# SwiGLU block in fp32: value and gate products split into three reduced-precision products, with the gating on GpSimd

## The chip, the cores and the metric

The kernel runs on one core of one Trainium2 chip. The metric is device time in microseconds (us). Engines in the profile: PE (TensorE, matmul), PEld (its weight loads), DVE (VectorE), ACT (ScalarE), POOL (GpSimd) and SP (SyncE, whose queue starts most transfers).

## The reference

A polysketch attention feeds a SwiGLU feed-forward block. q, k and v are fp32. The sketches S1, S2 and the three weights come as float64; the kernel narrows them to fp32 in its first 65 us (lines L216 to L239), beside the first batch.

```python
def phi(x):                                   # x: (4 batches, 4 heads, 1088, 32)
    a = np.einsum('rd,bhsd->bhsr', S1, x)     # r = 8
    b = np.einsum('rd,bhsd->bhsr', S2, x)
    return np.einsum('bhsi,bhsj->bhsij', a, b).reshape(*x.shape[:-1], r * r)
q_p, k_p = phi(q), phi(k)
kv = np.einsum('bhsf,bhsd->bhfd', k_p, v)
z = np.sum(k_p, axis=2)
num = np.einsum('bhsf,bhfd->bhsd', q_p, kv)
den = np.einsum('bhsf,bhf->bhs', q_p, z)[..., None] + 1e-06
x = (num / den).transpose(0, 2, 1, 3).reshape(4352, 128)

g = x @ w_gate                                # 128 x 1536
silu = g * (1.0 / (1.0 + np.exp(-g)))
val = x @ w_val                               # 128 x 1536
out = silu * val @ w_out                      # 1536 x 128
```

## The kernel before

The 4352 tokens stand as columns of `xT`, 128 partitions deep. Each batch of 1088 tokens is three blocks of 384, 384 and 320 columns; the 1536 hidden values are 12 chunks of 128. One chunk of one block is a *unit*: a gate product, a value product, Silu and the product of both, and later a *down* product that adds the unit to the block's sum. There are 144 units. An fp32 matmul of the program appears in the profile as two matmul instructions.

```python
    free_banks = ["g0", "g1", "g2", "acc"]      # one bank of 512 fp32 columns each
    def bank(tag=None):                         # round robin over the free banks
        if tag is None:
            tag = free_banks[turn[0] % len(free_banks)]
            turn[0] += 1
        return psum.tile([P, TB], FP32, tag=tag, name="bank")
    def wide(tag):                              # "a" and "b": two banks each, for the attention
        return psum.tile([P, 2, TB], FP32, tag=tag, name=tag)

    LAG = 2
    def unit(i, j, late=False, between=(None, None)):
        t0, n = blocks[i]
        g, u = bank(), bank()
        for o, w in ((g, wg), (u, wv)):
            ... # between
            nc.tensor.matmul(o[:, 0:n], w[:, j, :], xT[:, t0 : t0 + n], start=True, stop=True)  # L773
        sg = fpool.tile(...)
        nc.scalar.activation(sg[:, 0:n], g[:, 0:n], AF.Silu)                                   # L779
        ... # hj: a place of hbuf
        todo.append((i, j))
        ... # late units of the first batch: copied by ScalarE, multiplied on GpSimd (L796)
            nc.vector.tensor_tensor(out=hj[:, 0:n], in0=sg[:, 0:n], in1=u[:, 0:n], op=ALU.mult) # L790

    def down():
        i, j = todo.pop(0)
        ...
        nc.tensor.matmul(acc[i][:, 0:n], wo[:, j, :], hidden[i, j][:, 0:n],
                         start=(j == 0), stop=(j == NCH - 1))                                  # L804
        ...
        if j == NCH - 1:
            store(i, n)                         # VectorE transposes (L833), then the output's transfers
```

The attention of the later batches is a generator whose pieces are laid between the units: `parts_of(n)` lays n pieces, `group()` lays pieces up to the next point at which TensorE's attention products stand together, and those products. The pieces are mostly VectorE's: feature products (L324), spread products and sums (L679, L686), transposes (L710, L274, L509). The feature sums are GpSimd's (L494), the numerators TensorE's (L730).

```python
    while todo:                                 # end of the first batch
        for _ in range(min(3, len(todo))):
            down()
        if ahead[0] != "first":
            parts_of(1)
    ...
    for b in range(1, B):                       # batches 2 to 4
        for z in range(3 * NCH):
            i, j = z // NCH, z % NCH
            if (b, z) in ((1, NCH), (2, 0), (2, 2 * NCH)):
                group()
            unit(3 * b + ((0, 2, 1)[i] if b == B - 1 else i), j)
            for _ in range(2):
                if len(todo) > LAG:
                    down()
            parts_of(2 if b == 1 and z in (0, 4, 6, 7, 8) else 1)
    ps = wide("a")[:, 0, 0:D]
    for j in range(NCH):                        # the last 128 tokens, straight into the output's form
        if todo and j % 4 == 0:
            down()
        straight(ps, j)                                                                        # L819
```

Of the kernel before, what the change touches and what calls it, by code (L numbers as in the profile page):

```python
# [6 lines left out]

FP32 = mybir.dt.float32
I32 = mybir.dt.int32
U32 = mybir.dt.uint32  # L10
I64 = mybir.dt.int64
AF = mybir.ActivationFunctionType
ALU = mybir.AluOpType
# [5 lines left out]
def kernel(  # L19
# [28 lines left out]
    nc = tc.nc  # L48
# [9 lines left out]
    NCH = Dff // P  # L58
# [25 lines left out]
    free_banks = ["g0", "g1", "g2", "acc"]  # L84
    turn = [0]

    def bank(tag=None):
        if tag is None:
            tag = free_banks[turn[0] % len(free_banks)]
            turn[0] += 1  # L90
        return psum.tile([P, TB], FP32, tag=tag, name="bank")

    def wide(tag):
        return psum.tile([P, 2, TB], FP32, tag=tag, name=tag)

    nc.scalar.preload_act_table(AF.Silu)

# [157 lines left out]
    def run(*gens):  # L255
        for g in gens:
            for _ in g:
                pass
# [242 lines left out]
    def turns(b):  # L501

        for c in kpieces:
            turn_k(*c)
            if c[1] == NC and b + 1 < B:
                load_k(b + 1)
            yield
        for x0, x1 in ((0, 4 * kpieces[0][1]), (4 * kpieces[0][1], 4 * NC)):
            nc.vector.transpose(out=qT[:, x0:x1, :], in_=qld[:, x0:x1, :])  # L509
            if x1 == 4 * NC and b + 1 < B:  # L510
                load_q(b + 1)
            yield
# [19 lines left out]
    def attentions():  # L532

        yield from turns(1)
        kp, qp = wide("a"), wide("b")
        for ps, products in ((kp, key_products), (qp, query_sketches)):
            for i, c in enumerate(kpieces):
                products(ps[:, i, :], *c)
        ka = apool.tile([P, NC * H, R], FP32, tag="kas", name="kas")
        qab = apool.tile([P, 2, NC * H, R], FP32, tag="qab", name="qab", bufs=2)
        fac = None, qab

        def sketch(ps, i):  # L550
            c0, c1 = kpieces[i]
            return ps[:, i, 0 : 64 * (c1 - c0)].rearrange("p (x t r) -> p x t r", t=2, r=R)

        for i, (c0, c1) in enumerate(kpieces):
            nc.scalar.copy(ka[:, H * c0 : H * c1, :], sketch(kp, i)[:, :, 0, :])
        phk = apool.tile([P, NC, H, R, R], FP32, tag="phk", name="phk")
        for n, (i, c0, c1) in enumerate(((0, 0, 3), (0, 3, 5), (1, 5, 7), (1, 7, 9))):
            first = H * (c0 - kpieces[i][0])
            kb = sketch(kp, i)[:, first : first + H * (c1 - c0), 1, :]
            key_features(phk, (ka[:, H * c0 : H * c1, :], kb), c0, c1)  # L560
            if n < 2:
                q0, q1 = kpieces[n]
                nc.scalar.copy(
                    qab[:, :, H * q0 : H * q1, :], sketch(qp, n).rearrange("p x t r -> p t x r")
                )
            if n % 3 != 1:
                yield
        zs = feature_sums(phk)
        for i, _ in enumerate(turns(2)):
            if i % 2:  # L570
                yield
        kvz = wide("a")
        values(kvz[:, 0, :], phk, zs)
        kq = wide("b")
        fac2, copies = sketches([
            (0, NC - 1, kq[:, 0], kq[:, 1]),
            (NC - 1, NC, kvz[:, 1, 0 : 2 * F], kvz[:, 1, 2 * F : 4 * F]),
        ])
        spread = spread_out(1, kvz[:, 0, :])
        for _ in range(4):  # L580
            yield
            run_copies(copies, 1)
        step = query_step(1, fac, spread)
        yield from step(0, 3)
        numerators(1, spread, 0, 3)
        yield "first"
        yield from step(3, NC)
        phk = hbuf[:, NH - 6 :, :].rearrange("p s (n h i j) -> p (s n) h i j", h=1, i=R, j=R)
        phk = phk.rearrange("p (c h) o i j -> p c (h o) i j", h=H)
        yield from features(phk, fac2, ())  # L590
        zs = feature_sums(phk)
        yield from turns(3)
        yield "pe"
        numerators(1, spread, 3, NC)
        kv = bank()
        values(kv, phk, zs)
        kp, qp = wide("a"), wide("b")
        fac3, copies = sketches([(c0, c1, kp[:, i], qp[:, i]) for i, (c0, c1) in enumerate(kpieces)])
        spread = spread_out(2, kv)
        run_copies(copies, 2)  # L600
        yield
        run_copies(copies, 2)
        yield
        yield from features(phk, fac3, ())
        zs = feature_sums(phk)
        yield from query_step(2, fac2, spread)(0, NC)
        yield "pe"
        numerators(2, spread, 0, NC)
        kv = bank()
        values(kv, phk, zs)  # L610
        spread = spread_out(3, kv)
        for _ in range(4):
            yield
        yield from query_step(3, fac3, spread)(0, NC)
        yield "pe"
        numerators(3, spread, 0, NC)
        yield

    def run_copies(copies, n):
        for f, *args in copies[:n]:  # L620
            f(*args)
        del copies[:n]
# [139 lines left out]

    lates = []

    def unit(i, j, late=False, between=(None, None)):


# [3 lines that stand above are left out]
            if between[0] and w is wv:  # L771
                between[0]()
            nc.tensor.matmul(  # L773
                o[:, 0:n], w[:, j, :], xT[:, t0 : t0 + n], start=True, stop=True
            )
        sg = fpool.tile(
            [P, BW], FP32, tag="sgl" if late else "sg", name="sg", bufs=6 if late else 3
        )
        nc.scalar.activation(sg[:, 0:n], g[:, 0:n], AF.Silu)  # L779
        slot_of[i, j] = slots.pop(0)  # L780
        hj = hbuf[:, slot_of[i, j], :]
        hidden[i, j] = hj
        todo.append((i, j))
        if late:
            if between[1]:
                between[1]()
            nc.scalar.copy(hj[:, 0:n], u[:, 0:n])
            lates.append((hj[:, 0:n], sg[:, 0:n]))
        else:
            nc.vector.tensor_tensor(  # L790
                out=hj[:, 0:n], in0=sg[:, 0:n], in1=u[:, 0:n], op=ALU.mult
            )
# [5 lines left out]
    def down():  # L798

        i, j = todo.pop(0)  # L800
        n = SPLIT if i == LAST else blocks[i][1]
        if j == 0:
            acc[i] = bank("g1" if i == 1 else "acc")
        nc.tensor.matmul(  # L804
            acc[i][:, 0:n],
            wo[:, j, :],
            hidden[i, j][:, 0:n],
            start=(j == 0),
            stop=(j == NCH - 1),
        )  # L810
        if i != LAST:
            hidden.pop((i, j))
            slots.append(slot_of[i, j])
        if j == NCH - 1:
            store(i, n)

    def straight(ps, j):

# [130 lines left out]
    def parts_of(n):  # L949

        for _ in range(n):
            if ahead[0] not in ("pe", "end"):
                ahead[0] = next(att, "end")

    def group():
        while ahead[0] != "pe":
            ahead[0] = next(att)
        ahead[0] = next(att, "end")
# [42 lines left out]
    order = [(i, j) for i in range(3) for j in range(NCH)]  # L1001
    for z, (i, j) in enumerate(seq):
        if z == 17:
            free_banks.pop()
            turn[0] %= 4
        unit(i, j)
        for p in parts.get(z, ()):
            part(*p)
        if z in (24, 25, 26):
            catch_up()  # L1010
        if z == 6:
            load_k(1)
            load_v(1, [nc.sync] * 4)
            load_q(1)
        if z >= 17:
            todo.remove(order[0])
            todo.insert(0, order.pop(0))
            down()
        if z >= 17:
            parts_of(1)  # L1020
    todo.sort()
    while todo:
        for _ in range(min(3, len(todo))):
            down()
        if ahead[0] != "first":
            parts_of(1)
    while ahead[0] != "first":
        parts_of(1)

    slots[:] = range(NH - 6)  # L1030

    for b in range(1, B):
        for z in range(3 * NCH):
            i, j = z // NCH, z % NCH
            if (b, z) in ((1, NCH), (2, 0), (2, 2 * NCH)):
                group()
            unit(3 * b + ((0, 2, 1)[i] if b == B - 1 else i), j)
            for _ in range(2):  # L1040
                if len(todo) > LAG:
                    down()
            parts_of(2 if b == 1 and z in (0, 4, 6, 7, 8) else 1)
    ps = wide("a")[:, 0, 0:D]
    for j in range(NCH):
        if todo and j % 4 == 0:
# [40 lines left out]
```

## Time and profile before

| | |
|---|---|
| time, median of 3 (lowest, highest) | 305.9 us (305.71, 306.23) |
| span of the profiled execution | 304.3 us |
| batch 1 ends, its remaining downs included | 92.5 us |
| start of the first unit after the group in batch 2 | 120.1 us |
| attention products before batch 3 | 163.1 us |
| attention products within batch 3, for batch 4 | 212.2 us |
| the last 16 matmuls begin | 298.7 us |

The times of the stages are from the timeline of the profile. A busy share in the page is an average over the whole span; the view by windows gives busy times in stretches. In a line of a group, the count stands after the x, then the busy us, the mean ns of one, and the idle time of the engine just before, with what ended it. In a timeline line the first number is the start and the second the length; `x2` merges two instructions in a row. A matmul's length contains the drain of the array, so the pace of a stream of matmuls is the distance of their starts. An idle time is put down to the engine that released the instruction last.

### The profile page before, as it was taken

To read this page: it belongs to the slowest core of one execution; us is meant where nothing else is said; L and a number is where in the kernel's file an instruction comes from. 1 tells how busy PE (TensorE), PEld (TensorE's weight loads), DVE (VectorE), ACT (ScalarE), POOL (GpSimd) and SP (SyncE) were. 2 spreads that over 40 slices of the span, in tenths; PEclk is the share of its full clock that TensorE was granted. 3 is DMA by queue.
4 is the path that set the end of the run, shared out by engine and by line. 5 is a ranking of instruction groups with operands and counts; after the bars stand their busy time and mean duration, and the time that the engine had idled before them with its cause. 6 is when DMAs were issued, how large, how long until landed. Compare 5 with 4: busy or idle time off the path is not lost.

```text
span 304.3 us, 5402 instructions
## 1 busy us (share of the span) xinstructions
PE 298.0 (98%) x2179; PEld 190.3 (63%) x2179; DVE 170.0 (56%) x334; ACT 93.8 (31%) x219; POOL 37.9 (12%) x54
## 2 busy tenths in 40 slices
PE   8899999999999999999999999999999999999995
PEld 7545566657565556556666655555676556676664
DVE  3997988692536991788932478822423322333321
ACT  3566764422102222322222222222322222222230
POOL 3216222174000050070000000000000000000000
PEclk9999999999999999999999999999999999999999
DMA  7563490404511000400100200100100100100101
GB/s 195 150 193 106 119 302 7 149 15 149 113 28 22 0 2 22 108 0 0 26 3 2 49 0 0 28 0 0 23 5 0 22 1 2 26 0 2 21 0 26
DMA packets 26136, 14.57 MB, mean 48 GB/s; under 512 B 18688, under 2 KB 24192, under 8 KB 26112
## 3 DMA queue, kind: packets, MB, share of 16 engines
q1 hardware_dynamic: 25456, 14.13, 18.5%
q8 instruction: 17, 0.28, 0.4%
q10 hardware_dynamic: 656, 0.10, 0.2%
q14 instruction: 7, 0.06, 0.1%
HBM read 11.41 MB, written 2.23 MB: 45 GB/s over the span
## 4 chain that ended last, share of the span: by engine, by line
PE 97%; DVE 1%; issue 0%; ACT 0%
PE bank L773 58%; PE bank L804 28%; PE bank L194 2%; PE a L730 1%; PE b L289 1%; PE bank L335 1%; PE a L819 1%; PE a L301 1%; PE bank L348 0%; PE bank L301 0%; PE a L392 0%; PE a L444 0%; PE a L335 0%; PE b L301 0%; PE b L730 0%
## 5 line engine op out<-in xcount | busy, mean ns | idle before, releaser
L790 DVE TENSOR_TENSOR hbuf<-sg,bank 128x384 f32<-128x384 f32 (+1 forms) x138 | 72.9, 529 | 99.5 <-PE bank L773 97.7
L779 ACT ACTIVATE sg<-bank 128x384 f32<-128x384 f32 (+1 forms) x144 | 68.0, 473 | 163.1 <-PE bank L773 159.9
L773 PE MATMUL bank<-xT,wg 128*128 128x384 f32 (+1 forms) x288 | 112.5, 472 | 0.0
L773 PE MATMUL bank<-xT,wv 128*128 128x384 f32 (+1 forms) x288 | 111.5, 469 | 0.2 <-DVE wv L239 0.2
L804 PE MATMUL bank<-hbuf,wo 128*128 128x384 f32 (+2 forms) x288 | 105.1, 460 | 0.0
L773 PEld LDWEIGHTS bank<-xT,wv 128*128 128x128 f32 x288 | 54.5, 190 | 33.7 <-DVE hbuf L790 0.9
L804 PEld LDWEIGHTS bank<-hbuf,wo 128*128 128x128 f32 x288 | 54.6, 190 | 32.0
L773 PEld LDWEIGHTS bank<-xT,wg 128*128 128x128 f32 x288 | 53.7, 190 | 32.2 <-issue 1.6
L494 POOL TENSOR_TENSOR zs<-hbuf 128x1024 f32<-128x1024 f32 x2 | 4.7, 2359 | 51.6 <-DVE hbuf L324 37.6
L833 DVE STREAM_TRANSPOSE o<-bank 128x384 f32<-128x384 f32 (+2 forms) x12 | 6.6, 549 | 7.8 <-PE bank L804 7.4
L679 DVE TENSOR_TENSOR phq<-spread,qab 128x768 f32<-128x768 f32 x9 | 9.7, 1075 | 0.5 <-DMA spread<-spread 0.5
L221 ACT ACTIVATE exp<-exp,rebias 128x384 int32<-128x384 int32 (+3 forms) x15 | 8.3, 551 | 2.4 <-DVE exp L216 1.7
L710 DVE STREAM_TRANSPOSE phT<-phq 128x768 f32<-128x768 f32 x9 | 8.7, 968 | 0.1
L686 DVE TENSOR_REDUCE dot<-phq 128x96 f32<-128x768 f32 x9 | 8.5, 947 | 0.1
L324 DVE TENSOR_TENSOR phq<-qab 128x768 f32<-128x768 f32 x9 | 8.5, 942 | 0.0
L747 ACT COPY xT<-a 128x64 f32<-128x64 f32 (+3 forms) x7 | 2.3, 367 | 18.2 <-PE b L730 11.8
L224 DVE SCALAR_TENSOR_TENSOR exp<-raw,exp 128x384 int32<-128x384 int32 (+2 forms) x14 | 7.0, 503 | 0.0
L230 DVE SCALAR_TENSOR_TENSOR man<-raw,man 128x384 f32<-128x384 uint32 (+2 forms) x14 | 6.9, 493 | 0.0
L222 ACT ACTIVATE man<-man 128x384 f32<-128x384 int32 (+3 forms) x15 | 6.8, 452 | 0.0
L494 POOL TENSOR_TENSOR zs<-zs 128x512 f32<-128x512 f32 (+1 forms) x6 | 6.6, 1101 | 0.5
L239 POOL TENSOR_TENSOR wg<-man,exp 128x384 f32<-128x384 f32 (+1 forms) x5 | 4.0, 805 | 18.2 <-DVE man L230 14.0
L274 DVE STREAM_TRANSPOSE kT<-kld 128x384 f32<-128x384 f32 (+2 forms) x9 | 5.9, 688 | 0.3 <-DMA kld<-in_k_dram 0.3
(127 smaller groups left out, 161.4 us busy)
## 6 DMA issues: line engine op xcount, KB each, us to landing
kld<-in_k_dram SPq DMA_DIRECT2D x4, 544.0 KB, 4.3
vld<-in_v_dram SPq DMA_DIRECT2D x12, 144.0 KB, 5.1
qld<-in_q_dram SPq DMA_DIRECT2D x3, 544.0 KB, 4.2
raw<-in_moe_w_out_dram SPq DMA_DIRECT2D x4, 384.0 KB, 4.9
out_dram<-o SPq DMA_DIRECT2D x28, 48.0 KB, 1.9
raw<-in_moe_w_gate_dram SPq DMA_DIRECT2D x3, 384.0 KB, 3.6
raw<-in_moe_w_val_dram SPq DMA_DIRECT2D x3, 384.0 KB, 3.3
out_dram<-o SPq DMA_DIRECT2D x16, 40.0 KB, 1.7
```

Source lines behind the costliest of these rows:

```text
L221: nc.scalar.activation(e[:], e[:], AF.Relu, bias=rebias[: shape[0], :], scale=8.0)
L224: nc.vector.scalar_tensor_tensor(out=e[:], in0=hi, scalar=-(1 << 31), in1=e[:], op0=ALU.bitwise_and, op1=ALU.bitwise_or,)
L230: nc.vector.scalar_tensor_tensor(out=f, in0=lo, scalar=2.0**-52, in1=f, op0=ALU.mult, op1=ALU.add)
L324: engine.tensor_tensor(out=phk[:, c0:c1, :, :, :].rearrange("p c h i j -> p (c h) i j"), in0=ka.unsqueeze(3).to_broadcast([P, n, R, R]), i ...
L494: add = lambda o, a, b: nc.gpsimd.tensor_tensor(out=o, in0=a, in1=b, op=ALU.add)
L679: nc.vector.tensor_tensor(out=phq[:, c0:c1, :, :, :], in0=zrep.unsqueeze(1).to_broadcast([P, n, H, R, R]), in1=f.unsqueeze(3).to_broadcast ...
L686: nc.vector.tensor_reduce(out=dot[:, x, :], in_=phq[:, c0:c1, :, :, :].rearrange("p c h j i -> p (c h) j i"), axis=AX.X, op=ALU.add,)
L710: nc.vector.transpose(out=phT[:, :, :, c0:c1, :].rearrange("p h g c t -> p c (h g) t"), in_=phq[:, c0:c1, :, :, :].rearrange("p c h (g i) ...
L773: nc.tensor.matmul(o[:, 0:n], w[:, j, :], xT[:, t0 : t0 + n], start=True, stop=True)
L779: nc.scalar.activation(sg[:, 0:n], g[:, 0:n], AF.Silu)
L790: nc.vector.tensor_tensor(out=hj[:, 0:n], in0=sg[:, 0:n], in1=u[:, 0:n], op=ALU.mult)
L804: nc.tensor.matmul(acc[i][:, 0:n], wo[:, j, :], hidden[i, j][:, 0:n], start=(j == 0), stop=(j == NCH - 1),)
```

## The change

An fp32 number is cut into a part with 12 significant bits and a rest. The change's premise is that a matmul of type `float32r` multiplies such parts exactly. The value product is put together from three of them: with w = w1 + w0, x = x1 + x0 and beta = 4096, the parts are w1·x1, (beta·w0)·x0 and (w1 - beta·w0)·(x1 - beta·x0). A factor of 1 + 1/beta on the sum of the first two, and of -1/beta on the third, gives w1·x1 + w0·x1 + w1·x0 + w0·x0. The aim is to replace a full fp32 product on TensorE by three reduced ones, with the additions on engines that have time left.

In batches 2 and 3 the value product is split, in batch 4 the gate product too. Four units after two of the groups, and the last unit of all, stay as they were. The product of gate and value moves from VectorE to GpSimd in split units. Downs come up to five units after their unit, where it was two. From the 18th of the ordinary units of batch 1 on, banks are taken by age from all eight, of those that are not held, instead of round robin from three; the attention's double banks are held while it uses them.

```diff
+    PS = psum.tile([P, 8, TB], FP32, name="PS")
+    place = dict(g0=0, g1=1, g2=2, acc=3, a=4, b=6)
 ...
     def bank(tag=None):
-        if tag is None:
-            tag = free_banks[turn[0] % len(free_banks)]
+        if tag is not None:
+            i = place[tag]
+        elif oldest[0]:
+            i = min((i for i in used if i not in held), key=used.get)
+        else:
+            i = place[free_banks[turn[0] % len(free_banks)]]
             turn[0] += 1
 ...
+    def cut_weights(w):
+        for c, (w1, wb, wd) in enumerate(homes(w)):            # 4 pieces of 3 chunks
+            src = w[:, 3 * c : 3 * c + 3, :]
+            nc.scalar.activation(w1, src, AF.Copy, scale=CUT)
+            nc.gpsimd.tensor_tensor(out=low[:], in0=src, in1=whole(w1), op=ALU.subtract)
+            yield
+            nc.scalar.activation(wb, low[:], AF.Copy, scale=BETA)
+            nc.gpsimd.tensor_tensor(out=wd, in0=whole(w1), in1=whole(wb), op=ALU.subtract)
+            yield
+    def cut_tokens(i, engine=nc.gpsimd):
 ...
+        nc.scalar.activation(x1[:, 0:n], x, AF.Copy, scale=CUT)
+        engine.tensor_tensor(out=x0[:, 0:n], in0=x, in1=whole(x1[:, 0:n]), op=ALU.subtract)
+        yield
+        nc.vector.scalar_tensor_tensor(                        # xd = x1 - beta * x0
+            out=xd[:, 0:n], in0=whole(x0[:, 0:n]), scalar=-BETA, in1=whole(x1[:, 0:n]), ...)
+    def cut_unit(i, j, both=False):
 ...
+        for d, (_, _, wd) in zip(ds, parts):
+            nc.tensor.matmul(d, wd, xd, start=True, stop=True)
+        if not both:
+            nc.tensor.matmul(g, wg[:, j, :], xT[:, t0 : t0 + n], start=True, stop=True)
+        for w1, wb, _ in parts:
+            p = bank()[:, 0:n]
+            nc.tensor.matmul(p, w1, x1, start=True, stop=False)
+            nc.tensor.matmul(p, wb, x0, start=False, stop=True)
 ...
+        for d in ds:
+            nc.scalar.activation(s, d, AF.Copy, scale=-1.0 / BETA)
 ...
+        for p, s in zip(ps, sums):
+            nc.vector.scalar_tensor_tensor(
+                out=s, in0=p, scalar=1.0 + 1.0 / BETA, in1=s, op0=ALU.mult, op1=ALU.add)
+        nc.scalar.activation(sg, sums[0] if both else g, AF.Silu)
 ...
+        nc.gpsimd.tensor_tensor(out=hj[:, 0:n], in0=sg, in1=sums[-1], op=ALU.mult)
 ...
+    cutting = [cut_weights(wv), cut_weights(wg)]
     while todo:
 ...
+        for _ in range(2):
+            next(cutting[0], None)
 ...
+    line = [3 * b + k for b in range(1, B) for k in ((0, 2, 1) if b == B - 1 else range(3))]
+    END = len(line) * NCH
+    run(cut_tokens(line[0], nc.vector))
+    for y in range(END):
 ...
+        if (b, z) in ((1, NCH), (2, 0), (2, 2 * NCH)):
+            group()
+            if i not in x_parts:
+                run(cut_tokens(i, nc.vector))
+        if (b, z) in ((1, NCH), (1, NCH + 1), (2, 0), (2, 1)) or y == END - 1:
+            unit(i, j)
+        else:
+            cut_unit(i, j, both=b == B - 1)
+        lag = min(5, END - y + 1)
 ...
+        if b == 1 and z >= 3 * NCH - 18:
+            next(cutting[1], None)
+        if j == 4 and y // NCH not in (0, 2) and y + NCH < END:
+            coming_x = cut_tokens(line[y // NCH + 1])
+        if j in (4, 6):
+            next(coming_x, None)
```

## The prediction
> **What bounds the kernel now.** I read the page's engine totals and the chain of work that ended last first, since they say which engine's time is the kernel's time.
>
> ```profile
> PE 298.0 (98%) x2179; PEld 190.3 (63%) x2179; DVE 170.0 (56%) x334; ACT 93.8 (31%) x219; POOL 37.9 (12%) x54
> ...
> PE 97%; DVE 1%; issue 0%; ACT 0%
> ```
>
> TensorE is busy nearly all the time and is nearly all of the chain, so time is saved by giving it less to do and lost wherever it is made to wait. Next, the groups with shapes kept apart (line, engine, operation, count, then busy us and mean ns):
>
> ```profile
> L773 PE MATMUL bank<-xT,wg 128*128 128x384 f32 x192 | 78.5, 490 | 0.0
> ...
> L790 DVE TENSOR_TENSOR hbuf<-sg,bank 128x384 f32<-128x384 f32 x90 | 49.6, 551 | 63.0 <-PE bank L773 62.6 <-ACT sg L779 0.2
> L779 ACT ACTIVATE sg<-bank 128x384 f32<-128x384 f32 x96 | 47.2, 492 | 113.6 <-PE bank L773 110.4 <-DVE hbuf L790 3.2
> ...
> L796 POOL TENSOR_TENSOR hbuf<-hbuf,sg 128x384 f32<-128x384 f32 x6 | 5.9, 1003 | 0.0
> ```
>
> There are 96 units of 384 tokens and x192 matmuls: one fp32 matmul is two instructions. The mean of 490 ns contains the pipeline's drain; the pace is in the timeline (start, us, engine, ...):
>
> ```profile
> 251.28 0.81 PE L773 MATMUL bank<-xT,wv 128*128 128x384 f32 x2
> 251.48 0.49 ACT L779 ACTIVATE sg<-bank 128x384 f32<-128x384 f32 x1 [1.44 <-PE bank L773]
> 251.61 0.51 PEld L804 LDWEIGHTS bank<-hbuf,wo 128*128 128x128 f32 x2
> 251.93 0.81 PE L804 MATMUL bank<-hbuf,wo 128*128 128x384 f32 x2
> 252.20 0.56 DVE L790 TENSOR_TENSOR hbuf<-sg,bank 128x384 f32<-128x384 f32 x1 [1.38 <-PE bank L773]
> 252.25 0.51 PEld L773 LDWEIGHTS bank<-xT,wg 128*128 128x128 f32 x2
> 252.57 0.81 PE L773 MATMUL bank<-xT,wg 128*128 128x384 f32 x2
> ```
>
> Starts are 0.645 us apart, so one instruction takes 323 ns: two passes of 384 columns. A unit (gate, value, down) is 1.94 us. At 320 columns the same view gives 0.539 us a matmul, 1.62 a unit.
>
> Then the stages, in the view by windows (start:end, length, then busy us of PE, PEld, DVE, ACT, POOL):
>
> ```profile
> 92.50:116.00 23.50, 23.50 (x149) 13.63 (x151) 20.23 (x35) 6.01 (x13) 5.10 (x4) 1.00 0.05 8
> 116.00:143.00 27.00, 26.61 (x259) 16.85 (x248) 17.44 (x28) 7.83 (x19) 6.28 (x4) 1.00 0.16 37
> ...
> 187.00:211.00 24.00, 24.00 (x76) 14.20 (x75) 13.08 (x21) 5.89 (x12) 0.00 (x0) 1.00 0.06 9
> ...
> 276.00:298.20 22.20, 22.20 (x83) 14.92 (x82) 7.34 (x14) 5.89 (x12) 0.00 (x0) 1.00 0.05 8
> ```
>
> The average of 56% for VectorE hides that in the first stretch of the second batch (92.5 to 116) it is busy 20.2 of 23.5 us, while in the last batch (276 on) it is a third busy. The second batch is where an extra demand on it or on GpSimd can hurt. One more stretch of the timeline, for what happens when GpSimd and VectorE meet:
>
> ```profile
> 128.82 2.35 POOL L494 TENSOR_TENSOR zs<-hbuf 128x1024 f32<-128x1024 f32 x1 [14.02 <-PE bank L773]
> ...
> 129.46 0.55 DVE L790 TENSOR_TENSOR hbuf<-sg,bank 128x384 f32<-128x384 f32 x1 [0.78 <-PE bank L773]
> ...
> 129.93 2.06 DVE L679 TENSOR_TENSOR phq<-spread,qab 128x768 f32<-128x768 f32 x1
> ...
> 131.25 2.67 POOL L494 TENSOR_TENSOR zs<-zs 128x512 f32<-128x512 f32 x2
> ```
>
> L679 has a median of 951 ns; here it lasts 2.06, ending 0.8 after GpSimd's add ended at 131.17. The two GpSimd adds after it take 2.67 where an undisturbed pair takes 2.08 at 111.92. L790, with one operand in PSUM, is not slowed. So a VectorE operation with both operands in SBUF and a GpSimd operation exclude each other here.
>
> **What the Trainium skill says.** (1) "FP8 and Floating Point Precision", TensorE Precision Notes: true fp32 is four passes, reduced fp32 truncates the operand to about 22 bits. Two instructions of two passes agree with the four; a reduced matmul isn't in this trace. That it needs one pass is my inference: the built program after has 2317 matmul instructions against 2179, exactly one more for each of the 138 products that became three. (2) "TensorE: Matmul & The Clock Gate", Back-to-back issue gap: N/2.4 + 2.5 ns when warm. The trace agrees: 2 x 384/2.4 + 3 = 323. (3) "ScalarE: Activation LUTs", What ACT_TABLE_LOAD costs: 186 + 0.833 N ns, 506 at 384, and neighbours overlap by 93. The trace has 492 and starts of neighbours about 0.1 us closer than their lengths. (4) "GPSIMD Engine Reference", Specifications: its SBUF interfaces are shared with VectorE, with contention from instructions that have two SBUF inputs. The stretch just shown agrees, with 1.1 us lost by one of them.
>
> **The change, part by part.**
>
> *Removed from TensorE.* One reduced product is an estimated 384/2.4 + 3 = 163 ns, three are 489 against 646: 157 ns less. At 320 columns it is 3 x 136 = 408 against 539: 131 less. The weight loads should not be the limit: the last 16 matmuls (L819, 128 columns) begin about 0.11 us apart with a load each, and 0.11 is under 0.136. In batches 2 and 3 all but four units have a split value: 44 of 384 columns and 24 of 320, 44 x 0.157 + 24 x 0.131 = 10.1 us. In the last batch all but one unit have both split: 23 x 0.314 + 12 x 0.262 = 10.4 us. Sum: 20.5 us, a time of 285.4 if nothing waits.
>
> *Added elsewhere.* Each split product costs ScalarE one copy from PSUM (0.49) and VectorE one multiply-add (about the 0.55 of L790, whose place it takes for the value). The product with the gate goes to GpSimd, 1.00 us a unit by L796. Cutting the weights: 8 steps of ScalarE and 8 of GpSimd for each matrix; those of the value lie in the 15 us of down products before 92.5 and are hidden. Cutting tokens: 0.49 ScalarE, 0.5 to 1.0 on VectorE or GpSimd, 0.55 VectorE for each of nine blocks.
>
> *Last batch.* TensorE needs 6 x 0.163 + 0.646 = 1.62 us a unit. ScalarE has copy, copy, Silu, and the Silu waits for VectorE's sum: 0.49 + 0.04 + 0.55 + 0.04 + about 0.45 = 1.57, as the second copy lies beside the sum. At 320 columns: 1.36 against about 1.40. Balanced, so most of the 10.4 is kept; I take 1 us off, and 0.7 for the longer chain at the very end.
>
> *Middle batch (third).* GpSimd 1.0 and ScalarE 0.98 of 1.785 us, VectorE 13 of 24 us: kept.
>
> *Second batch, first stretch.* The cut of the first tokens stands on VectorE behind the store of the batch before (L833, 92.70 to 93.22), then two operations, so the first split product starts near 94.3 instead of 92.5, and VectorE's first sum near 95.6. From its first unit on, at 94.06, VectorE had 19.3 us of unbroken work in the kernel before. The work is the same now, with some 2 us for ten exclusions by GpSimd: 95.6 + 19.3 + 2 = 117, where it was 113.4. GpSimd's sums (5.6 us) follow. So the unit after the group starts near 121.7, where it was 120.1, with three more down products (1.9 us) still owed. Against the gain of 1.9 counted above this is a loss of about 5.4 us.
>
> *Second batch, second stretch.* For some thirteen units GpSimd has 13 products, one sum of 5.6, eight weight cuts and a token cut: 27.5 us, and some 5 us of VectorE's exclusive work between them. TensorE takes about 22. Downs five units behind give 5 x 1.785 less the chain of about 2.5, some 6.4 us, of slack: 32.5 - 22 - 6.4, a stall of 4. A ScalarE cut of the gate waits for GpSimd's step before it, which can pass the lag on to the sums; within the 4.
>
> *Banks.* The units now use the two double banks as well, so the attention products wait for a multiply-add to free them: an estimated 0.3 us at five places, 1.5.
>
> Sum: 305.9 - 20.5 + 1.7 + 5.4 + 4 + 1.5 = 298. The schedule has slack that I can't follow by hand, and the losses are counted one by one as if none covered another; I go one below, to 297.
>
> **The rivals.** *All of it lands* (TensorE stays the bound, 286 to 289): for it, 97% of the chain and the lag of five units; against it, VectorE's unbroken 19.3 us. *GpSimd and VectorE become the bound in the second batch* (about 297, my main line; 303 to 306 if the exclusions double): for it, the 2.06 us of L679; against it, that GpSimd's product starts just after VectorE has begun its next operation, which hides part. *Reduced products at half rate or with exposed weight loads*: at two passes a split costs three times 0.323 = 0.97 against 0.646, 138 x 0.3 = 42 us more, about 345. Against it, one instruction for each product; I give it 3%.
>
> **Range and chances.** The range spans the first rival's upper end to the second with doubled losses: 289 to 305. Under 299.8 is faster by 2%: most of the middle and all of the first rival, 0.68. Within 2%: 0.28. Slower: 0.04, almost all from the third.
>
> **What would show it.** Right: split products 0.163 us apart; TensorE's busy sum about 20 us less; idle TensorE time almost only between 92 and 165, waiting for VectorE before the first group and for GpSimd's products in the second stretch; the last batch near 1.62 and 1.4 us a unit. Wrong: starts over 0.2 us apart (a weight load or a second pass); a last batch clearly over 1.7 us a unit (ScalarE's chain); no idle time in the second batch (I overrated the exclusions, and it lands near 288); idle time in the third batch, which I take to be free of it.

## The result, and the profile after

The changed kernel takes 307.7 us (median of 4; 307.31 to 308.19) where the kernel before takes 305.8 beside it. The ratio is 1.006, with a 95% interval of 1.0046 to 1.0075. The prediction was 297, with a range of 289 to 305.

The page of the changed kernel, its engine totals, then the granted clock in 40 slices, then the shares of the chain of work that ended last:

```profile
PE 288.5 (94%) x2317; PEld 207.1 (68%) x2317; DVE 198.2 (65%) x381; ACT 163.1 (53%) x382; POOL 167.5 (55%) x179
...
PEclk9999999999999999999797999999999999999999
...
PE 78%; POOL 9%; DVE 7%; issue 2%; DMA 2%; ACT 1%; SPq 0%; DVEq 0%; POOLq 0%
```

TensorE's busy sum fell by 9.5 us, but its share of the chain fell from 97% to 78%: GpSimd and VectorE now stand in it. Two slices near the middle of the span no longer show the full clock (7, with a 9 between them). The new groups, with shapes kept apart (count, then busy us and mean ns):

```profile
L888 DVE SCALAR_TENSOR_TENSOR sum<-PS,sum 128x384 f32<-128x384 f32 x90 | 47.8, 552 | 29.9 <-ACT sum L885 13.4 <-PE PS L880 9.3 <-POOL hbuf L897 6.6
L885 ACT ACTIVATE sum<-PS 128x384 f32<-128x384 f32 x90 | 41.4, 486 | 25.2 <-PE PS L873 25.0
L897 POOL TENSOR_TENSOR hbuf<-sg,sum 128x384 f32<-128x384 f32 x67 | 76.0, 1140 | 54.8 <-DVE sum L888 29.8 <-ACT sg L892 12.7 <-ACT sum L885 11.3
```

The sum and the copy last what was assumed (0.55 and 0.49). GpSimd's product averages 1.14 against the 1.00 of an undisturbed one. The pace of the last batch, TensorE alone (start, us, line):

```profile
285.13 0.33 PE L879 MATMUL PS<-x,w 128*128 128x384 f32 x1
285.30 0.34 PE L880 MATMUL PS<-x,wb 128*128 128x384 f32 x1
285.48 0.70 PE L940 MATMUL PS<-hbuf,wo 128*128 128x320 f32 x2
...
286.19 0.34 PE L873 MATMUL PS<-xd,wd 128*128 128x384 f32 x1
```

Reduced products begin about 0.174 us apart at 384 columns (0.146 at 320), so one pass each, a little over the assumed 0.163 and 0.136. The down in these lines belongs to a block of 320 columns, five units behind. Four places of the program divide the span:

| us | before | after | difference since the last place |
|---|---|---|---|
| first numerators (end of batch 1) | 88.8 | 91.2 | +2.4 |
| first unit after the group in batch 2 | 120.1 | 124.7 | +2.2 |
| attention products before batch 3 | 163.1 | 175.6 | +7.9 |
| end of the span | 304.3 | 306.5 | -10.3 |

The gain arrives in batches 3 and 4 and is given back earlier. The longest loss is the second stretch of batch 2, from the group to batch 3: 43.0 us before, 50.9 after. By windows (start:end, length, busy us of PE, PEld, DVE, ACT, POOL, then the clock):

```profile
124.70:143.30 18.60, 18.60 (x75) 12.46 (x68) 12.76 (x18) 8.24 (x18) 11.33 (x10) 1.00 0.23 50
143.30:165.00 21.70, 15.96 (x52) 10.70 (x52) 15.94 (x25) 9.79 (x26) 20.51 (x20) 0.85 0.01 1
...
276.00:298.20 22.20, 22.20 (x117) 20.17 (x116) 14.44 (x29) 17.65 (x42) 14.15 (x15) 1.00 0.06 8
```

All of it lies between 143.3 and 165: TensorE works 16.0 of 21.7 us, at a mean clock of 0.85, while GpSimd is busy for 20.5 of them. In the stretch shown of the last batch TensorE has no idle time. The timeline where TensorE first stops, all engines:

```profile
142.15 0.88 POOL L855 TENSOR_TENSOR x<-xT,x 128x320 fp32r<-128x320 f32 x1
142.97 2.21 POOL L897 TENSOR_TENSOR hbuf<-sg,sum 128x384 f32<-128x384 f32 x2
143.06 1.27 DVE L859 SCALAR_TENSOR_TENSOR xd<-x,x 128x320 fp32r<-128x320 f32 x1 [3.61 <-POOL x L855]
...
144.84 0.44 PE L873 MATMUL PS<-xd,wd 128*128 128x384 f32 x1 [1.49 <-DVE sum L888]
145.14 0.99 POOL L840 TENSOR_TENSOR low<-wg,graw 128x384 f32<-128x384 f32 x1
...
146.16 0.52 ACT L842 ACTIVATE graw<-low 128x384 fp32r<-128x384 f32 x1 [6.85 <-POOL low L840]
146.59 0.47 ACT L885 ACTIVATE sum<-PS 128x384 f32<-128x384 f32 x1
...
147.12 0.91 PE L875 MATMUL PS<-xT,wg 128*128 128x384 f32 x2 [1.84 <-ACT sum L885]
```

Up to 142.15 GpSimd had been in the feature sum (L523), and products and cuts had queued behind it. Two engines then stand behind GpSimd. VectorE waits 3.61 us for a token cut (L855) with a unit's sum behind it in its queue, and TensorE waits for that sum (1.49). ScalarE waits 6.85 us for the step of the gate cut on GpSimd (L840), with the copies out of PSUM (L885) behind it, and TensorE waits for the bank that such a copy frees (1.84). TensorE stops once more from 159.2 to 161.6 (2.41, again for L885). The waits, summed (times, longest):

```profile
ACT graw L842 <- POOL low L840: 14.3, 4, 6.8
```

Twice after these stops TensorE runs at half its clock, each time for 3.41 us:

```profile
148.24:151.65 3.41, 3.41 (x8) 2.18 (x7) 1.95 (x3) 1.32 (x5) 3.41 (x4) 0.50 0.00 0
161.89:165.30 3.41, 3.41 (x9) 2.21 (x9) 3.40 (x7) 1.78 (x6) 3.15 (x4) 0.50 0.03 7
```

The first of these periods begins 1.1 us after the end of the second stop, the other 0.3 us after the end of the third. An ordinary gate product of 384 columns has a length of 0.81 at 141.55 and 1.48 at 149.78. Two times 3.41 us at half the clock make TensorE's own work 3.4 us longer, beside 5.7 us of idle time in the second stretch.

### The profile page after: what moved, and what is told of

It reads as the page before. It is cut to its first block, busy times and chain, and to the rows that moved or that the text cites. A ratio compares the mean times of both kernels' runs of the same rounds, so it can differ in the third digit from the quotient of the medians.

```text
span 306.5 us, 6266 instructions
## 1 busy us (share of the span) xinstructions
PE 288.5 (94%) x2317; PEld 207.1 (68%) x2317; DVE 198.2 (65%) x381; ACT 163.1 (53%) x382; POOL 167.5 (55%) x179
## 4 chain that ended last, share of the span: by engine, by line
PE 78%; POOL 9%; DVE 7%; issue 2%; DMA 2%; ACT 1%; SPq 0%; DVEq 0%; POOLq 0%
PE PS L940 24%; PE PS L907 15%; PE PS L875 11%; PE PS L873 7%; PE PS L880 7%; PE PS L879 7%; POOL zs L523 4%; POOL hbuf L897 3%; PE PS L330 2%; DMA kld<-in_k_dram 2%; PE PS L768 1%; POOL low L840 1%; DVE hbuf L353 1%; PE PS L318 1%; PE PS L364 1%
## 5 line engine op out<-in xcount | busy, mean ns | idle before, releaser
L897 POOL TENSOR_TENSOR hbuf<-sg,sum 128x384 f32<-128x384 f32 (+1 forms) x103 | 108.9, 1062 | 74.6 <-DVE sum L888 42.9
L940 PE MATMUL PS<-hbuf,wo 128*128 128x384 f32 (+2 forms) x288 | 106.0, 464 | 0.6 <-DVE hbuf L924 0.6
L888 DVE SCALAR_TENSOR_TENSOR sum<-PS,sum 128x384 f32<-128x384 f32 (+1 forms) x138 | 70.2, 529 | 55.8 <-POOL hbuf L897 21.4
L885 ACT ACTIVATE sum<-PS 128x384 f32<-128x384 f32 (+1 forms) x138 | 61.0, 469 | 35.1 <-PE PS L873 34.8
L940 PEld LDWEIGHTS PS<-hbuf,wo 128*128 128x128 f32 x288 | 52.1, 190 | 10.5 <-DVE hbuf L924 1.2
L875 PE MATMUL PS<-xT,wg 128*128 128x384 f32 (+1 forms) x136 | 53.9, 479 | 4.2 <-ACT sum L885 4.2
L873 PE MATMUL PS<-xd,wd 128*128 128x384 f32 (+1 forms) x103 | 50.8, 493 | 4.5 <-DVE sum L888 2.7
L879 PE MATMUL PS<-x,w 128*128 128x384 f32 (+1 forms) x103 | 53.0, 515 | 0.0
L892 ACT ACTIVATE sg<-PS 128x384 f32<-128x384 f32 (+1 forms) x68 | 32.1, 472 | 12.9 <-PE PS L875 10.0
L913 ACT ACTIVATE sg<-PS 128x384 f32<-128x384 f32 (+1 forms) x41 | 19.4, 476 | 28.3 <-PE PS L907 25.9
L907 PE MATMUL PS<-xT,wg 128*128 128x384 f32 (+1 forms) x82 | 32.8, 482 | 0.0
L875 PEld LDWEIGHTS PS<-xT,wg 128*128 128x128 f32 x136 | 24.5, 193 | 11.6 <-ACT sum L885 4.9
L907 PEld LDWEIGHTS PS<-xT,wg 128*128 128x128 f32 x82 | 14.7, 189 | 10.1 <-issue 1.2
```

The lines of the kernel that those rows point to most:

```text
L873: nc.tensor.matmul(d, wd, xd, start=True, stop=True)
L875: nc.tensor.matmul(g, wg[:, j, :], xT[:, t0 : t0 + n], start=True, stop=True)
L879: nc.tensor.matmul(p, w1, x1, start=True, stop=False)
L885: nc.scalar.activation(s, d, AF.Copy, scale=-1.0 / BETA)
L888: nc.vector.scalar_tensor_tensor(out=s, in0=p, scalar=1.0 + 1.0 / BETA, in1=s, op0=ALU.mult, op1=ALU.add)
L892: nc.scalar.activation(sg, sums[0] if both else g, AF.Silu)
```

## The experiments

Three theories. *Queue order*: engines work their queues in order, and a cheap step that waits for GpSimd's backlog holds up ScalarE's and VectorE's copies and sums behind it. *Capacity*: GpSimd and VectorE, which exclude each other, simply have too much to do in batch 2, wherever each step stands. *Banks and pace*: the rest comes from taking banks by age, and from reduced products that are longer than assumed.

**The gate cuts one batch later.** Same work, moved to batch 3.

```diff
-        if b == 1 and z >= 3 * NCH - 18:
+        if b == 2 and z >= 6:
             next(cutting[1], None)
```

> The gate weights are cut in batch 3 (from its seventh unit on) instead of in the second half of batch 2. Theory 1 (queue order: ScalarE stands behind a cut step that waits for GpSimd, TensorE runs out of sums and its clock halves after the stall): the stalls at 143 to 165 us go, 7 to 9 us less, about 300. Theory 2 (GpSimd simply has too much work in batch 2, with VectorE's exclusions): also 6 to 8 us less, since 8 us of GpSimd leave batch 2. Theory 3 (the loss lies before 125 us and in the length of the reduced products): no change, 307.

Measured: 303.2 us, ratio to before 0.9885 (0.9841 to 0.993). The second stretch of batch 2 fell from 50.9 to 43.4, at full clock; batch 3, up to its attention products for batch 4, rose from 46.3 to 49.1, where the same ScalarE wait now adds up to 8.0 us in 4 times. The gate cuts are what makes the stretch long, but moving them takes work off GpSimd too, so it doesn't tell order from capacity. The stop of 1.49 us for VectorE's sum, behind the token cut, stays.

**The gate cuts in place, their two halves apart.** Every step stays in batch 2; ScalarE's and GpSimd's second step of a piece come four to seven units after the first, and `low` has tiles of its own, where it shared those of the sums.

```diff
+    def finish(x):
+        wb, low, wd, w1 = x
+        nc.scalar.activation(wb, low[:], AF.Copy, scale=BETA)
+        nc.gpsimd.tensor_tensor(out=wd, in0=whole(w1), in1=whole(wb), op=ALU.subtract)
 ...
-            low = fpool.tile([P, 3, P], FP32, tag="sgl", name="low", bufs=6)
+            low = fpool.tile([P, 3, P], FP32, tag="lowb", name="low", bufs=2)
 ...
-            nc.scalar.activation(wb, low[:], AF.Copy, scale=BETA)
-            nc.gpsimd.tensor_tensor(out=wd, in0=whole(w1), in1=whole(wb), op=ALU.subtract)
+            later.append((wb, low, wd, w1))
+            yield
+            ... # for the gate, two to three more yields
+            finish(later.pop(0))
             yield
```

> The gate weights are still cut in batch 2, with the same 16 steps on the same engines, but ScalarE's second step of a piece stands four or five units after GpSimd's first step, so it should find its input ready. Theory 1: most of the stall goes, about 302. Theory 2: GpSimd has the same work in the same batch, so 306 to 308 remain. Theory 3: 307.

Measured: 301.9 us, 0.9841 (0.9788 to 0.9894). The stretch, by windows of this kernel:

```profile
144.50:166.00 21.50, 18.47 (x79) 13.20 (x78) 18.05 (x30) 12.14 (x30) 21.50 (x20) 1.00 0.07 10
```

One line of its timeline, and one of its waits, summed over the whole span:

```profile
160.89 0.78 PE L955 MATMUL PS<-hbuf,wo 128*128 128x320 f32 x2 [1.35 <-POOL hbuf L912]
...
ACT sg L907 <- POOL hbuf L912: 13.9, 14, 3.6
```

GpSimd is busy 21.5 of 21.5 us, and yet the second stretch takes 44.8 instead of 50.9: the same work on the same engine (37.5 us busy in the whole stretch, 37.9 in the change), 6.1 us less. ScalarE's waits for the gate cut are gone (what is left, 6.3 us, belongs to the value cut in batch 1), and the clock is 1.00. This is for queue order and against capacity as the main cause. The edit also takes `low` out of the tiles of the sums. In the change's trace the copies into these tiles (L885, 384 columns) wait for TensorE in 25.0 of their 25.2 us, not for a tile, so the order is the likelier of the two; no run separates them. Two longer stops of TensorE are left in the stretch, neither of which lowers the clock: 1.49 us for VectorE's sum, and 1.35 for a down that waits for GpSimd's product (L912). ScalarE still stands behind GpSimd too, but less: a Silu waits for one of the three `sg` tiles that GpSimd's products hold.

**Batch 2 not split.** The work of batch 2 as before, lag and banks as in the change.

```diff
-        if (b, z) in ((1, NCH), (1, NCH + 1), (2, 0), (2, 1)) or y == END - 1:
+        if b == 1 or (b, z) in ((2, 0), (2, 1)) or y == END - 1:
             unit(i, j)
```

> The units of batch 2 stay whole fp32 products with VectorE's multiply, as before the change; batches 3 and 4 are split as in the change, and all cuts stay where they are. From the attention products before batch 3 to the end the change took 10.3 us less than the kernel before, and the end of batch 1 2.4 us more. Theories 1 and 2: all losses of batch 2 go, 305.8 - 10.3 + 2.4 = 298. Theory 3 (losses elsewhere): over 302.

Measured: 295.4 us, 0.9633 (0.9589 to 0.9677). That is 12.3 us less than the change. By the prediction's figures the 34 split products of batch 2 were to take 22 x 0.157 + 12 x 0.131 = 5.0 us off TensorE; with all that comes with them they cost 12.3 net. The second stretch takes 43.3 with TensorE never idle.

**The old banks in batch 1.** Round robin from three in batch 1, by age only from batch 2 on.

```diff
         if z == 17:
-            oldest[0] = True
+            free_banks.pop()
+            turn[0] %= 4
             hold("acc")
 ...
+    oldest[0] = True          # before batch 2
```

> The ordinary units of batch 1 take their banks round robin from three, as before the change; by age only from batch 2 on. If the 2.4 us by which batch 1 ended later come from units that now wait for a bank of the attention, 2 to 2.5 us go, about 305.5. If they come from the cutting of the value weights that lies there, nothing changes, 307.5.

Measured: 305.5 us, 0.9983 (0.9967 to 0.9999), 2.3 below the change. The first numerators are back at 88.9 (91.2 in the change, 88.8 before): all that batch 1 lost was the order of the banks. It brings nothing there, as batch 1 has no split products.

**Both of these.** The edits of the last two together: only batches 3 and 4 are split.

```diff
+        if b == 1 or (b, z) in ((2, 0), (2, 1)) or y == END - 1:
 ...
+    oldest[0] = True          # before batch 2
```

> Batch 2 whole, as in the run before, and the old banks in batch 1. If the two repairs are independent, 295.4 - 2.25 = 293.2.

Measured: 293.6 us, 0.9589 (0.9575 to 0.9603). The old banks still bring 1.8 of their 2.3 us here, so the two losses are nearly independent.

**Half of batch 2 split.** First block whole; the other two split; old banks in batch 1; gate cuts beside the whole units, no token cut for the first block; the token cut of the third block on VectorE.

```diff
 ... # old banks, as above
-    run(cut_tokens(line[0], nc.vector))
 ...
-        if (b, z) in ((1, NCH), (1, NCH + 1), (2, 0), (2, 1)) or y == END - 1:
+        if (b == 1 and z < NCH + 2) or (b, z) in ((2, 0), (2, 1)) or y == END - 1:
 ...
-        if b == 1 and z >= 3 * NCH - 18:
+        if b == 1 and z < NCH:
             next(cutting[1], None)
 ...
-            coming_x = cut_tokens(line[y // NCH + 1])
+            coming_x = cut_tokens(line[y // NCH + 1], nc.vector if b == 1 else nc.gpsimd)
```

> The old banks in batch 1; the first of batch 2's three blocks whole, the other two split as in the change; the gate weights cut beside that first block, where GpSimd has little to do; the tokens of the third block cut on VectorE instead of on GpSimd behind its feature sum. Theory 1 (order of queues): the second stretch of batch 2 then has GpSimd's products and one sum but nothing that another engine's queue stands behind, so its 22 split products keep their gain of about 0.11 us each: 293.2 - 2.4 = 291. Theory 2 (capacity with exclusions): the second stretch still stalls, 294 to 297.

Measured: 294.5 us, 0.962 (0.9606 to 0.9635): 0.9 more than without. The gate cuts beside the first block end that block 2.1 us later. The second stretch takes 42.1 against 43.3 unsplit, so half of the 2.4 us (10 x 0.124 + 12 x 0.101) is kept. TensorE's busy time in it falls by 1.9 (41.4 for 43.3), and one stop of 0.79 takes most of the rest, where a down waits for VectorE's transposes of a finished block (L971):

```profile
152.48 0.78 PE L940 MATMUL PS<-hbuf,wo 128*128 128x320 f32 x2 [0.79 <-DVE o L971]
```

Earlier in the stretch VectorE and GpSimd hold each other up, by windows and in the timeline:

```profile
125.00:135.00 10.00, 10.00 (x41) 6.96 (x39) 9.60 (x12) 5.75 (x12) 7.50 (x5) 1.00 0.33 74
```

```profile
130.98 3.08 POOL L523 TENSOR_TENSOR zs<-hbuf 128x1024 f32<-128x1024 f32 x1
131.75 2.65 DVE L855 TENSOR_TENSOR x<-xT,x 128x320 fp32r<-128x320 f32 x1
```

VectorE is busy 9.6 of 10 us, and part of that is standing: the cut that it now does itself lasts 2.65 us beside GpSimd's sum, and the sum 3.08, where an undisturbed one took 2.35. But TensorE works 10.0 of these 10 us, so nothing is lost there yet. That VectorE's backlog from here causes the later stop is not shown.

**A lag of two.** The kernel that splits batches 3 and 4 only, with downs two units behind.

```diff
-        lag = min(5, END - y + 1)
+        lag = 2
```

> As e_plain_banks (batch 2 whole, old banks in batch 1), with the downs two units behind instead of five. From the end of a unit's products to GpSimd's result it takes about 0.17 + 1.0 + 0.5 + 1.0 = 2.7 us in batch 4; two units less a down are 2 x 1.58 - 0.65 = 2.5 us. If that is the rule, TensorE waits 0.2 to 0.5 us a unit in batch 4, 35 units, 8 to 15 us more: about 303. If the chain is hidden anyway: 293.

Measured: 295.9 us, 0.9661 (0.9647 to 0.9676), 2.2 over the one with five. So the lag is worth little, far from what one of the readings expected. Part of what it shows on the way is not slack at all: with two units three downs fewer are owed at each place, so the attention products before batch 3 come 3.5 us later (164.3 for 160.8) and the end only 2.2.

**The gate product on VectorE.** Again against the kernel that splits batches 3 and 4 only.

```diff
-        nc.gpsimd.tensor_tensor(out=hj[:, 0:n], in0=sg, in1=sums[-1], op=ALU.mult)
+        nc.vector.tensor_tensor(out=hj[:, 0:n], in0=sg, in1=sums[-1], op=ALU.mult)
```

> As e_plain_banks, with the product of gate and value on VectorE instead of GpSimd in batches 3 and 4. VectorE then needs 3 x 0.55 less overlaps of 0.07, 1.45 us of the 1.58 us a unit in batch 4, and in batch 3 one operation more beside the attention. If GpSimd is needed to keep VectorE from becoming the bound: 298 or more. If VectorE has the room: 293, with a shorter tail.

Measured: 305.4 us, 0.9982 (0.9966 to 0.9997), 11.8 more. Batch 3, where VectorE still has attention pieces for batch 4, grows from 46.3 to 54.6 us, what follows from 84.6 to 88.2. A stretch of batch 3 (VectorE is third of the busy times) with the product on GpSimd and then on VectorE, and the longest stop there:

```profile
178.00:200.00 22.00, 22.00 (x87) 15.62 (x86) 17.02 (x29) 12.12 (x25) 15.30 (x13) 1.00 0.06 10
```

```profile
178.00:200.00 22.00, 19.13 (x74) 12.96 (x72) 20.82 (x36) 10.95 (x23) 1.28 (x1) 0.98 0.00 1
...
201.52 1.65 PE L940 MATMUL PS<-hbuf,wo 128*128 128x384 f32 x2 [4.39 <-DVE o L971]
```

VectorE is busy 20.8 of 22 us, and a down waits 4.39 us for its transposes of a finished block. GpSimd is needed, and the multiplication there is not the mistake.

**The third product in bf16.** The kernel that splits batches 3 and 4 only, with `xd` and `wd` stored as bf16. They are rounded to fewer bits, so the third product is no longer exact; its share in the result is divided by 4096.

```diff
+            wd = wd.bitcast(mybir.dt.bfloat16)[:, :, 0:P]
+        xd = xd[:].bitcast(mybir.dt.bfloat16)
+        x_parts[i][2] = xd
```

> As e_plain_banks, with the operands of the third reduced product (the one weighted by 1/4096) in bf16 instead of float32r. Reduced products stand 0.174 us apart at 384 columns where N/2.4 + 3 gives 0.163. If the 0.011 comes with 4-byte operands or their weight loads, the products of this kind take 0.163 and about 104 x 0.01 = 1 us goes, 292.6. If it is a cost of every single-pass product, the distance stays at 0.174 and the time at 293.6.

Measured: 292.3 us, 0.9549 (0.9527 to 0.9572), 1.3 less. In its timeline:

```profile
264.00 0.33 PE L876 MATMUL PS<-xd,gphq 128*128 128x384 bf16 x1
264.16 0.33 PE L876 MATMUL PS<-xd,wd 128*128 128x384 bf16 x1
...
264.50 0.34 PE L883 MATMUL PS<-x,graw 128*128 128x384 f32 x1
264.68 0.34 PE L882 MATMUL PS<-x,w 128*128 128x384 f32 x1
```

The bf16 product takes 0.16, what the prediction assumed; the reduced fp32 one 0.17 to 0.18. The excess comes with the operands of four bytes. A weight load is recorded with 0.10 us in bf16 and 0.19 in fp32, but weights and tokens were changed together, so which of the two it is stays open.

**Half split, gate cuts late.** The kernel with half of batch 2 split, but the gate cuts spread over the end of batch 3.

```diff
-        if b == 1 and z < NCH:
+        if b == 2 and z >= 18 and z % 2 == 0:
             next(cutting[1], None)
```

> As f_half (first block of batch 2 whole, the other two split, third block's tokens cut on VectorE), with the gate weights cut late in batch 3, a step every second unit, instead of beside the first block of batch 2. In f_half that block ended 2.1 us later than in e_plain_banks, and the stretch after it took 1.2 us less. If the cuts were the cause of the 2.1: 294.5 - 2.1 = 292.4, under every kernel so far. If not: 294.5.

Measured: 292.2 us, 0.9545 (0.9522 to 0.9568), 2.4 less than with the cuts in the first block. GpSimd has room for them at the end of batch 3.

**The whole change, only the order altered.** All products split and all cuts made as in the change, but at other places: old banks in batch 1, gate cuts late in batch 3, the token cut of the third block on VectorE.

```diff
         if z == 17:
-            oldest[0] = True
+            free_banks.pop()
+            turn[0] %= 4
 ...
+    oldest[0] = True          # before batch 2
 ...
-        if b == 1 and z >= 3 * NCH - 18:
+        if b == 2 and z >= 18 and z % 2 == 0:
             next(cutting[1], None)
 ...
-            coming_x = cut_tokens(line[y // NCH + 1])
+            coming_x = cut_tokens(line[y // NCH + 1], nc.vector if b == 1 else nc.gpsimd)
```

> The change in full, batch 2 split throughout, with three placements altered only: old banks in batch 1, gate weights cut late in batch 3 at every second unit, third block's tokens of batch 2 cut on VectorE. The work of every engine is that of the change. Theory 1: the second stretch of batch 2 falls from 50.9 us to about 42, 305.5 - 8.5 = 297; what is left over e_plain_banks is the first stretch. Theory 2: over 301.

Measured: 297.7 us, 0.972 (0.9691 to 0.9748), 10.0 us less than the change. Not quite all work stays on its engine: the one token cut moves from GpSimd to VectorE, and with the gate cuts GpSimd's busy time in the second stretch falls from 37.9 to 29.5 us. So this run alone doesn't tell order from capacity either. The later half of the stretch, up to the attention products before batch 3, by windows:

```profile
143.00:165.00 22.00, 21.21 (x96) 15.56 (x97) 15.94 (x29) 12.06 (x29) 16.49 (x16) 1.00 0.06 10
```

The second stretch takes 42.1 instead of 50.9. TensorE idles 0.8 us in it, not 5.7, and never loses the clock: 4.9 of idle and 3.4 of clock make 8.3 of the 8.8 in TensorE's own account. The runs divide the 8.8 step by step: 6.1 go when only the gate cuts' halves are moved apart (44.8), 1.4 more when these cuts leave batch 2 (43.4), and 1.3 more with the token cut on VectorE (42.1). What is left to the kernel that doesn't split batch 2 lies in the first stretch: the unit after the group starts at 122.7, there at 117.5. Twelve products split before the group gain 12 x 0.124 = 1.5 and cost 5.2 net.

**All that helped.** Half of batch 2 split, old banks in batch 1, gate cuts late, third product in bf16 (with the rounding told above).

```diff
+        if (b == 1 and z < NCH + 2) or (b, z) in ((2, 0), (2, 1)) or y == END - 1:
 ...
+        if b == 2 and z >= 18 and z % 2 == 0:
 ...
+        xd = xd[:].bitcast(mybir.dt.bfloat16)
```

> j_half_late with the bf16 third product of i_bf16_third. If the two gains are independent: 292.2 less 1.3, and 22 more products at 0.01, so 290.7. If VectorE, saturated in the second stretch of batch 2, is what sets that stretch, the 22 bring nothing there: 291 to 291.5.

Measured: 291.3 us, 0.9508 (0.9482 to 0.9534), faster than both kernels: 4.9% below the kernel before, and 16.4 us below the change. The second stretch takes 42.1, as without bf16 (42.2), so the 22 more products of this kind bring nothing there.

## Why the prediction was wrong, point by point

**The step that failed: the second stretch of batch 2.** The prediction said "a stall of 4", and of the right mechanism: "A ScalarE cut of the gate waits for GpSimd's step before it, which can pass the lag on to the sums; within the 4." It was not within the 4. The stretch was to take 43.0 - 3.14 + 4 = 43.9 and took 50.9, 7.0 more. The estimate weighed GpSimd's work against the slack of five units that the downs have. The runs show that it was the wrong slack. In the change no down waited for GpSimd's product. The copies and sums waited for GpSimd's cuts, through ScalarE's and VectorE's queues, and behind them stand banks, which have no five units to give. With the two halves of a cut apart, the stretch took 6.1 us less beside a full GpSimd. Only then does the path show that the prediction counted on: one down waits for a product, 1.35 us where 4 were put down.

The prediction didn't have the halved clock at all. It makes TensorE's work 3.4 us longer, but how much of the loss that is stays open, as GpSimd, busy 20.5 of 21.7 us, may have held TensorE anyway. The mean clocks of single executions hint at a small share. With one slow period instead of two (a mean of 0.994 instead of 0.987 to 0.989) the change took 307.3 us once, and 307.6 to 308.2 otherwise. The kernel with the old banks, which has much the same stops, took 305.35 instead of 305.47 (medians of 5 and 13). A period adds 1.7 us to TensorE's work, and in these executions 0.1 to 0.9 us to the time.

**The reduced products: mechanism right, size off.** One pass each, as inferred. But 0.174 and 0.146 us instead of 0.163 and 0.136 make a split product save 0.124 and 0.101 us instead of 0.157 and 0.131. The term of 20.5 becomes 44 x 0.124 + 24 x 0.101 + 2 x (23 x 0.124 + 12 x 0.101) = 16.0. Of the missing 4.5, 0.7 lies in the second stretch and is counted above; 3.8 are left.

**Banks: place wrong, 0.9 short.** 1.5 us were put down for five places; 2.4 were lost in batch 1 alone, through the order of the banks in a part without any split products.

**The first stretch of batch 2: right within 0.6.** With the 2.4 of batch 1 added, the first split product was expected at 96.7 (96.8), the first sum at 98.0 (98.3), and the unit after the group at 124.1 (124.7). VectorE's unbroken work is the right account: from 98.3 to 119.2, 20.9 us where it was 19.3, with 1.6 us of stretching where 2 were put down. No run that splits the products of this stretch removes its loss; with only the order altered, 5.2 us remain.

**Last batch: 1.7 us of losses that did not come.** A unit of 384 tokens with a down of 384 columns takes 1.69 us (252.92 to 254.61), and 320 with 320 takes 1.41 (274.89 to 276.30). That is what the reduced products' real length makes of the predicted 1.62 and 1.36, TensorE without idle time. The 1 and 0.7 us were for ScalarE's chain and the tail. Batches 3 and 4 gain 10.3 where the products count 22 x 0.124 + 12 x 0.101 + 8.1 = 12.1. The 1.8 between are mostly the three downs that batch 2 leaves to batch 3 (3 x 0.645 = 1.9).

Together, 297 + 7.0 + 3.8 + 0.9 + 0.6 - 1.7 = 307.6, for 307.7 measured. The terms are read from the stages of one timeline, so that their sum closes is no proof of the causes, and the 1 us that the prediction took off its sum of 298 for losses that cover each other isn't among them.

**The rivals.** The one in which GpSimd and VectorE become the bound of batch 2 was the main line, and its upper end (303 to 306) rested on doubled exclusions. The exclusions did not have to double: the queues did it. The half rate of reduced products fell by the pace in the timeline. And the kernel with everything landing, 286 to 289, isn't reached by any version run: the term of the products itself is 4.5 short, and the first stretch of batch 2 loses in every run that splits its products.

## What to carry to other kernels

A cheap step on a lightly loaded engine that waits for a backlogged one hands the whole backlog to everything behind it in its queue: count what stands behind each wait between engines, and lay such a step several units after its producer. Slack counts only on the path that waits; five units of lag for the downs were worth 2.2 us and protected neither the copies nor the banks. And look at the stage, not at the share: where the helper already works unbroken (VectorE in the first stretch of batch 2), work taken off TensorE for 1.5 us cost 5.2.

## What the runs showed of the hardware

**The clock.** The Trainium skill, "TensorE: Matmul & The Clock Gate", section "What's actually happening", gives the half rate after an idle window of about 3.4 us. The traces show it after less idleness. In the change it came once after stops of 1.49 and 1.84 us with one product between, once after 2.41, and lasted 3.41 us each time. With the old banks it came during the second of two stops of 1.48 and 1.83 us and lasted 6.83. With the multiply on VectorE, in a stop of 4.39, it lasted 6.83 too. A lone stop of 1.49 us left the clock at 1.00.

**Exclusion.** Of two operations on VectorE and GpSimd, each with both operands in SBUF, each can be stretched: VectorE's subtraction to 2.65 us at 320 columns (0.52 at 384, at 95.52 in the change), GpSimd's 1024-column sum from 2.35 to 3.08. VectorE's sum with one operand in PSUM stays at 0.55.

**The reduced fp32 product.** One instruction and one pass, as its pace shows, but 0.174 us at 384 columns where bf16 takes 0.16.
